# First MLP layer of two chunks with tokens stationary, and a new order of scores and values on TensorE

## The chip, the cores and the metric

The kernel runs on one core of a Trainium2 chip. The metric is the device time of one execution in microseconds; the median over the runs is compared. Inside a core, TensorE (PE for matmuls, PEld for its weight loads), VectorE (DVE), ScalarE (ACT) and GpSimd (POOL) each work through their own instructions in order, and SyncE (SP) issues the DMAs in order. An instruction waits on semaphores for its inputs and for its output buffer.

## The reference, cut to what matters

```python
# q, k, v: (8, 8, 576, 64) float32; w_in: (512, 2048); w_out: (2048, 512)
scores = scale * np.matmul(q, k.transpose(0, 1, 3, 2))          # scale = 1/8
kth = np.partition(scores, -32, axis=-1)[..., -32:-31]
scores = np.where(scores >= kth, scores, -1e9)
scores = scores - np.max(scores, axis=-1, keepdims=True)
attn = np.exp(scores)
attn = attn / (np.sum(attn, axis=-1, keepdims=True) + 1e-09)
x = np.matmul(attn, v)                 # then (batch, seq, heads * 64) = (4608, 512)
h = x @ w_in
out = np.maximum(0.01 * h, h) @ w_out  # (4608, 512)
```

Attention keeps, in each row of 576 scores, the 32 largest; its output goes through a two-layer MLP with a leaky ReLU. The MLP's weights arrive as 64-bit words and are rounded to fp32 on the chip.

## The kernel before

**Units and steps.** Attention is cut into 144 units. A unit is 128 rows of queries of one pair of heads, or the last 64 rows of two pairs. The loop of L416 makes one step per unit, and each step works on several units at different stages: the top-k of unit s on DVE (`top_k`, L209), the mask of unit s-1 on POOL and its exponential on ACT, the normalization of unit s-2 on ACT and its transposition (`transpose`, L252: two copies that split the 16-bit halves, a DMA to DRAM and a transposing DMA back into `wT`). In even steps the scores of units s+2 and s+3 are computed (`scores`, L191) and the values of units s-4 and s-3 (`weigh_values`, L276), which `keep_values` (L290) copies into `x`. DVE's `reciprocals` of a step need the row sums `ze` that ACT makes at the end of the step before.

**MLP.** Tokens are cut into chunks, two of 128 and 17 of 256 (`CHUNKS`, L51). A chunk becomes ready when the values of all its units are there: chunk 0 in step 6, chunk 1 in step 10, chunk 2 in step 18, and then one every 8 steps (`ready_at`). The generator `mlp` (L299) emits a chunk's work in small pieces: for each of 16 groups of 128 hidden features four matmuls with the weights stationary and the tokens moving (`ph`), and a leaky ReLU by ACT into `gT[f]`; then for each 128 tokens 16 matmuls with `gT[f]` stationary (`pz`), a copy and a store. `mlp_steps` is called seven times in each step and takes pieces up to a budget. `slot_budget` (L379) divides the outstanding work, in the costs of `mlp_cost`, by the slots left until the next chunk is ready. So the order on each engine is written out by hand; nothing is reordered later (`tc.manual_schedule`). What ACT has to do for the MLP stands in ACT's queue between the parts of attention.

**Order in an even step on TensorE.** Five slots of MLP, the scores of the first new unit, the values of two units, the scores of the second new unit, two slots of MLP.

**PSUM.** There are 8 banks. Scores have two tiles `psc0` and `psc1` of two banks, one for each of the unit's heads, and both units of an even step use the same two. Values have one bank (`po`), the MLP three in turn (`ph`, `pz`). An fp32 matmul appears in the profile as two records.

**Tile shapes.** MLP matmuls use all 128 rows and 128 columns of the array, scores 64 rows (the head's dimension) and 128 columns, two heads in different rows, and values 128 rows and 64 columns, two heads in different columns.

**Rounding.** Before the loop, 16 pieces of weights are rounded, in three overlapped stages (`round_weights`, L103): ACT copies the parts out of the words, DVE makes scale and mantissa and TensorE sums the parts in PSUM, DVE multiplies. For odd pieces ACT makes `scale` (L127), for even ones DVE (L131). The loop of L400 also emits the loads of q and k, and at `n == NPIECE - 2` the scores of units 0 and 1.

Of the kernel before, what the change touches and what calls it, by code (L numbers as in the profile page):

```python
# [8 lines left out]
F32 = mybir.dt.float32  # L9
U32 = mybir.dt.uint32  # L10
U16 = mybir.dt.uint16
# [8 lines left out]
def kernel(  # L20
# [24 lines left out]
    B = NPAIR // HP  # L45
    HS = S // 2
    NFC = DFF // P
    WCH = 1024
# [14 lines left out]
    ps_sc = ctx.enter_context(tc.tile_pool(name="ps_sc", bufs=1, space=bass.MemoryType.PSUM))  # L63
    ps_po = ctx.enter_context(tc.tile_pool(name="ps_po", bufs=1, space=bass.MemoryType.PSUM))
    ps_ml = ctx.enter_context(tc.tile_pool(name="ps_ml", bufs=3, space=bass.MemoryType.PSUM))

# [8 lines left out]
    w_out = [const.tile([P, 4, DMODEL], F32, name=f"w_out{c}") for c in range(NFC // 4)]  # L75
    gT = [const.tile([P, CHMAX], F32, name=f"gT{f}") for f in range(NFC)]

# [25 lines left out]
    def round_weights(n):  # L103
# [21 lines left out]
        nc.vector.tensor_scalar(scale, scale, 1151.0, 896.0, ALU.min, ALU.max)  # L125
        if n % 2:
            nc.scalar.activation(scale, scale, AF.Copy, bias=-896.0 * 128, scale=128.0)  # L127
        nc.vector.tensor_scalar(m_top, top, 0xF, 0x3F80, ALU.bitwise_and, ALU.bitwise_or)
        nc.vector.tensor_scalar(top, top, 0x8000, None, ALU.bitwise_and)
        if n % 2 == 0:  # L130
            nc.vector.tensor_scalar(scale, scale, 896.0, 128.0, ALU.subtract, ALU.mult)  # L131
        if n < NPIECE - 3:
            pw = ps_sc.tile([P, 2, 512], F32, name=f"psc{n % 2}")
            sums = [(pw[:, h, :], h * 512) for h in range(2)]
            ends = [(pw.rearrange("p h n -> p (h n)"), 0)]
        else:
            ends = sums = [(ps_ml.tile([P, 512], F32, name="pw", tag="ml"), h * 512) for h in range(2)]
# [52 lines left out]

    def scores(u):  # L191
        ps = [ps_sc.tile([P, 2, 512], F32, name=f"psc{i}") for i in range(2)]
        for n in range(0, len(u.parts), 2):
            for half in range(2):
                for i, pi, side, r0 in u.parts[n:n + 2]:
                    qt, kt = qk_of[pi]
                    d = slice(side * D, (side + 1) * D)
                    nc.tensor.matmul(  # L198
                        ps[i][r0:r0 + u.rows, half, 0:HS],
                        qt[d, u.q0:u.q0 + u.rows],  # L200
                        kt[d, half * HS:(half + 1) * HS],
                        start=True, stop=True,
                    )
        u.both = work.tile([P, 2, S], F32, name="s_sb", bufs=5)
        u.s = [u.both[:, i, :] for i in range(2)]
        for i in range(2):
            nc.scalar.copy(u.s[i].rearrange("p (h n) -> p h n", h=2), ps[i][:, :, 0:HS])  # L207

# [81 lines left out]
    def keep_values(u, po):  # L290
# [5 lines left out]
        for o, (pi, _, _) in enumerate(u.outs):  # L296
            nc.scalar.copy(x_of[ch][pi % HP][:, col:col + n], po[:, o, :])  # L297

    def mlp(ch):  # L299

        n = CHUNKS[ch]
        t0 = sum(CHUNKS[:ch])
        x = x_of[ch]
        for f in range(NFC):
            ph = ps_ml.tile([P, 512], F32, name="ph", tag="ml")
            for c in range(HP):
                nc.tensor.matmul(  # L307
                    ph[:, 0:n], w_in[c][:, f * P:(f + 1) * P], x[c][:, 0:n],
                    start=(c == 0), stop=(c == HP - 1),
                )  # L310
                if c == 1:
                    yield 2 * max(n, 225)
            nc.scalar.activation(gT[f][:, 0:n], ph[:, 0:n], AF.Prelu, alpha=SLOPE)  # L313
            yield 2 * max(n, 225)
        for r0 in range(0, n, P):
            m = min(P, n - r0)
            pz = ps_ml.tile([P, 512], F32, name="pz", tag="ml")
            for f in range(NFC):
                nc.tensor.matmul(  # L319
                    pz[0:m, 0:DMODEL], gT[f][:, r0:r0 + m], w_out[f // 4][:, f % 4, :],  # L320
                    start=(f == 0), stop=(f == NFC - 1),
                )
                if f % 2 and f + 1 < NFC:
                    yield 2 * DMODEL
# [5 lines left out]
    def mlp_cost(ch):  # L330
        n = CHUNKS[ch]
        return NFC * HP * max(n, 225) + -(-n // P) * NFC * DMODEL

# [45 lines left out]
    def slot_budget(s):  # L379

        after = [at for at, _ in ready_at if at >= s]
        until = after[0] if after else s
        return backlog[0] / ((until + 1 - s) * SLOTS)

    SLOTS = 7

    with tc.manual_schedule():
# [12 lines left out]
        for n in range(NPIECE + 2):  # L400
# [6 lines left out]
            if 6 <= n < 6 + HP:  # L407
                load_qk(n - 6)
            elif n == NPIECE - 2:
                for u in steps[0:2]:  # L410
                    scores(u)
            elif n == NPIECE - 1:
                load_v(0)
                load_v(1)

        for s in range(len(steps) + LAG + 1):  # L416
# [29 lines left out]
            if old:  # L446
                exponents(old, 1)
                sums(old)
            for u in new[:1]:
                scores(u)  # L450
            if s % 2 == 0:
                po = ps_po.tile([P, 2, P], F32, name="po")
                for values in (weigh_values, keep_values):
# [3 lines left out]
                attended(s)  # L457
            for u in new[1:]:
                scores(u)
            budget = slot_budget(s + 1)  # L460
# [62 lines left out]
```

## Time and profile before

| What | Value |
|---|---|
| Median of 9 runs | 1516.41 us (1515.33 to 1518.45) |
| Profiled execution: time / span | 1518.21 us / 1516.4 us |
| Busy PE, DVE, ACT, POOL | 1430.6, 1330.6, 1117.7, 1078.1 us |
| PE L307 (first layer), L319 (second layer) | 519.7, 506.7 us |
| PE L198 (scores), L283 (values) | 198.2, 180.3 us |
| ACT L313 (leaky ReLU), L207 (copies of scores), L259 (splits) | 107.1, 169.3, 315.7 us |
| Idle of PE before L198, waiting for L207 | 29.8 us, the longest 23.4 |
| Idle of DVE, waiting for `ze` | 75.2 us in 48 places |
| Mean granted TensorE clock | 0.973 |

The span goes from the first to the last instruction. A matmul's recorded time contains its passage through the array, so records overlap: the distance between starts tells what one costs. A group is named by line, engine, operation and output<-inputs; a wait is put down to what ended it.

### The profile page before, as it was taken

The page shows a single profiled execution, that of the slowest core. Times are in us where ns is not written, and L with a number is a line of the kernel's source. Part 1 is how long each engine was busy: PE and PEld are TensorE (multiplying, and loading weights), DVE is VectorE, ACT ScalarE, POOL GpSimd, SP SyncE. Part 2 cuts the span into 40 slices and gives each one's busy share as a digit, 9 for nine tenths or more (in the row PEclk, how much of TensorE's full clock was granted, in tenths as well). Part 3 has the DMA queues.
Part 4 walks back from the last instruction along what each step waited for, and adds up shares of the span by engine and source line. Part 5 has one row for each costly group of instructions (what it writes and reads, how often), then busy time and mean ns, then how long its engine had stood idle before and what let it go on. Part 6 is the DMA issues. An engine that isn't in the chain of part 4 may idle for free.

```text
span 1516.4 us, 24441 instructions
## 1 busy us (share of the span) xinstructions
PE 1430.6 (94%) x8192; PEld 952.4 (63%) x8192; DVE 1330.6 (88%) x3421; ACT 1117.7 (74%) x2141; POOL 1078.1 (71%) x726
## 2 busy tenths in 40 slices
PE   6736978999999999999999999999999999999998
PEld 2324665757575767575757676767676666666774
DVE  6799999999999999999999998999999989999600
ACT  7846786878787877687878787878787878787720
POOL 0068778787878777878787877777787878788700
PEclk9966999999999999999999999999999999999999
DMA  7714456555665455545754456555665455544510
GB/s 287 277 31 125 126 162 165 166 141 148 179 159 148 126 170 158 160 137 148 182 165 134 139 158 170 164 136 147 190 158 147 135 158 155 156 130 142 141 53 14
DMA packets 399294, 227.05 MB, mean 150 GB/s; under 512 B 343360, under 2 KB 343360, under 8 KB 397120
## 3 DMA queue, kind: packets, MB, share of 16 engines
q1 hardware_dynamic: 399168, 225.49, 53.5%
q8 instruction: 64, 1.05, 0.3%
q14 instruction: 62, 0.51, 0.1%
HBM read 46.14 MB, written 94.37 MB: 93 GB/s over the span
## 4 chain that ended last, share of the span: by engine, by line
PE 83%; DVE 11%; ACT 3%; DMA 1%; issue 1%; SPq 0%; POOL 0%; DVEq 0%; ACTq 0%; POOLq 0%
PE ph L307 32%; PE pz L319 30%; PE psc L198 10%; PE po L283 10%; DVE tops L221 4%; DVE pairs L224 3%; DVE pairs L216 1%; ACT split L259 1%; DVE scale L144 1%; DVE w_in L147 0%; ACT s_sb L238 0%; ACT s_sb L250 0%; DVE w_out L147 0%; DMA raw<-in_weights_dram 0%; ACT scale L127 0%
## 5 line engine op out<-in xcount | busy, mean ns | idle before, releaser
L234 POOL TENSOR_SCALAR pen<-s_sb,tops 128x576 f32<-128x576 f32 x288 | 637.5, 2214 | 240.2 <-DVE tops L221 204.2
L221 DVE MAX8 tops<-pairs 128x8 f32<-128x288 f32 (+1 forms) x1152 | 635.8, 591 | 0.0
L307 PE MATMUL ph<-x,w_in 128*128 128x256 f32 (+1 forms) x2432 | 519.7, 374 | 6.4 <-ACT gT L313 6.4
L319 PE MATMUL pz<-w_out,gT 128*128 128x512 f32 x1152 | 506.7, 595 | 1.3 <-ACT gT L313 1.3
L307 PEld LDWEIGHTS ph<-x,w_in 128*128 128x128 f32 x2432 | 444.4, 193 | 87.4 <-issue 21.9
L224 DVE MATCH_REPLACE8 pairs<-tops,pairs 128x288 f32<-128x288 f32 (+1 forms) x864 | 460.0, 537 | 0.0
L235 POOL TENSOR_TENSOR s_sb<-s_sb,pen 128x576 f32<-128x576 f32 x288 | 406.4, 1411 | 24.1
L319 PEld LDWEIGHTS pz<-w_out,gT 128*128 128x128 f32 x1152 | 215.9, 190 | 265.5 <-issue 263.0
L259 ACT COPY split<-s_sb 128x1152 uint16<-128x1152 uint16 x288 | 315.7, 1145 | 0.0
L207 ACT COPY s_sb<-psc 128x576 f32<-128x576 f32 x288 | 169.3, 639 | 114.3 <-PE psc L198 114.3
L250 ACT ACTIVATE s_sb<-s_sb,rz 128x576 f32<-128x576 f32 x288 | 206.7, 767 | 35.4 <-DVE rz L247 35.4
L238 ACT ACTIVATE s_sb<-s_sb,nbias 128x576 f32<-128x576 f32 x288 | 221.2, 768 | 11.4 <-POOL s_sb L235 11.4
L198 PE MATMUL psc<-kt,qt 64*128 64x288 f32 (+1 forms) x1280 | 198.2, 438 | 29.8 <-ACT s_sb L207 29.8
L216 DVE TENSOR_TENSOR pairs<-s_sb 128x576 f32<-128x576 f32 x288 | 213.5, 780 | 10.2 <-ACT split L259 0.5
L283 PE MATMUL po<-wT,vt 128*64 128x128 f32 (+1 forms) x3200 | 180.3, 269 | 21.4 <-DMA wT<-apart 20.6
L283 PEld LDWEIGHTS po<-wT,vt 128*64 128x64 f32 x3200 | 161.4, 139 | 53.0 <-issue 27.2
L313 ACT ACTIVATE gT<-ph 128x256 f32<-128x256 f32 (+1 forms) x304 | 107.1, 368 | 102.0 <-PE ph L307 101.6
L198 PEld LDWEIGHTS psc<-kt,qt 64*128 64x128 f32 (+1 forms) x1280 | 111.0, 181 | 101.1 <-ACT s_sb L207 39.0
L232 POOL TENSOR_SCALAR nbias<-tops 128x2 f32<-128x2 f32 x144 | 33.4, 232 | 92.1 <-DVE tops L221 79.3
L247 DVE RECIPROCAL rz<-ze 128x2 f32<-128x2 f32 x144 | 22.4, 156 | 75.7 <-ACT ze L243 75.2
L297 ACT COPY x<-po 128x128 f32<-128x128 f32 (+1 forms) x160 | 32.4, 264 | 63.2 <-PE po L283 63.0
L224 DVE MATCH_VALUE_LOAD pairs<-tops,pairs 128x8 f32 x864 | 62.2, 72 | 0.0
(38 smaller groups left out, 317.8 us busy)
## 6 DMA issues: line engine op xcount, KB each, us to landing
apart<-split SPq DMA_DIRECT2D x288, 288.0 KB, 2.1
raw<-in_weights_dram SPq DMA_DIRECT2D x16, 1024.0 KB, 5.1
vt<-in_vk_dram SPq DMA_DIRECT2D x32, 320.0 KB, 3.7
qt<-in_qT_dram SPq DMA_DIRECT2D x32, 288.0 KB, 3.8
kt<-in_kT_dram SPq DMA_DIRECT2D x32, 288.0 KB, 4.0
out_dram<-o_sb SPq DMA_DIRECT2D x36, 256.0 KB, 2.0
wT<-apart SPq DMA_TRANSPOSE x144, 4.6
```

What stands on the lines that cost most here:

```text
L198: nc.tensor.matmul(ps[i][r0:r0 + u.rows, half, 0:HS], qt[d, u.q0:u.q0 + u.rows], kt[d, half * HS:(half + 1) * HS], start=True, stop=True,)
L216: nc.vector.tensor_tensor(pairs[:, :, n, :], u.both[:, :, 0:HS], u.both[:, :, HS:S], op)
L221: nc.vector.max(out=u.tops[:, i, r, :], in_=rest[i])
L224: nc.vector.match_replace(out=rest[i], in_to_replace=u.tops[:, i, r, :], in_values=rest[i], imm_value=LOWEST)
L234: nc.gpsimd.tensor_scalar(pen, u.s[i], u.tops[:, i, ROUNDS - 1, 7:8], MASKED, ALU.is_lt, ALU.mult)
L235: nc.gpsimd.tensor_tensor(u.s[i], u.s[i], pen, ALU.add)
L238: nc.scalar.activation(u.s[i], u.s[i], AF.Exp, bias=u.nbias[:, i:i + 1], scale=SCALE, accum_out=u.z[:, i:i + 1])
L250: nc.scalar.activation(u.s[i], u.s[i], AF.Copy, bias=0.0, scale=u.rz[:, i:i + 1])
L259: nc.scalar.copy(split, pairs[:, :, h])
L283: nc.tensor.matmul(po[side * D:(side + 1) * D, o, :], vt[:, c, side, :], u.wT[:, c + side * NKC if c + 1 < NKC else c, r:r + n], start=(c ...
L307: nc.tensor.matmul(ph[:, 0:n], w_in[c][:, f * P:(f + 1) * P], x[c][:, 0:n], start=(c == 0), stop=(c == HP - 1),)
L319: nc.tensor.matmul(pz[0:m, 0:DMODEL], gT[f][:, r0:r0 + m], w_out[f // 4][:, f % 4, :], start=(f == 0), stop=(f == NFC - 1),)
```

## The change

Three things are done, and some that they need.

- In `scores`, both units of an even step are computed together. A row's 576 scores are split into 352 (`wide`) and 224 (`narrow`) columns. A unit has a `wide` tile of two banks; both share the two banks of `narrow`. The order on PE is first unit wide, first narrow, second narrow, second wide, and ACT copies in that order. The values' `po` has no bank of its own: it takes a buffer of `wide`, of which there are two. In the even step, values and their copies now come first, then all scores.
- The first layer of chunks 0 and 1 (`hidden_of_few`) has the 128 tokens stationary and 512 weights moving. Its output has tokens in partitions, so after the leaky ReLU TensorE transposes it in blocks of 128x128, and ACT copies four of them at a time into `gT`. `mlp_cost` gives these chunks another cost, and `slot_budget` spreads their work over one step less.
- The scores of units 0 and 1 are emitted one piece later in the rounding loop, behind the copies of the last piece. That piece's `scale` is made by DVE, and where DVE makes it, it now precedes the mantissa.
- The MLP has two PSUM buffers in place of three. For the other chunks one buffer holds two groups of 256 columns and one ReLU evicts both. `gT` is one tile.

```diff
--- before.py
+++ after.py
@@ -44,6 +44,8 @@
     HP = DMODEL // P
     B = NPAIR // HP
     HS = S // 2
+    NARROW = 224
+    WIDE = S - NARROW
     NFC = DFF // P
     WCH = 1024
     LEFT = S % P
@@ -61,8 +63,7 @@
     small = ctx.enter_context(tc.tile_pool(name="small", bufs=5))
     halves = ctx.enter_context(tc.tile_pool(name="halves", bufs=3, space=bass.MemoryType.DRAM))
     ps_sc = ctx.enter_context(tc.tile_pool(name="ps_sc", bufs=1, space=bass.MemoryType.PSUM))
-    ps_po = ctx.enter_context(tc.tile_pool(name="ps_po", bufs=1, space=bass.MemoryType.PSUM))
-    ps_ml = ctx.enter_context(tc.tile_pool(name="ps_ml", bufs=3, space=bass.MemoryType.PSUM))
+    ps_ml = ctx.enter_context(tc.tile_pool(name="ps_ml", bufs=2, space=bass.MemoryType.PSUM))
 
     ident = const.tile([P, P], F32, name="ident")
     make_identity(nc, ident)
@@ -73,7 +74,7 @@
 
     w_in = [const.tile([P, DFF], F32, name=f"w_in{c}") for c in range(HP)]
     w_out = [const.tile([P, 4, DMODEL], F32, name=f"w_out{c}") for c in range(NFC // 4)]
-    gT = [const.tile([P, CHMAX], F32, name=f"gT{f}") for f in range(NFC)]
+    gT = const.tile([P, NFC, CHMAX], F32, name="gT")
 
 
 
@@ -123,14 +124,14 @@
         nc.vector.tensor_scalar(scale, top, 4, 0x7FF, ALU.logical_shift_right, ALU.bitwise_and)
 
         nc.vector.tensor_scalar(scale, scale, 1151.0, 896.0, ALU.min, ALU.max)
-        if n % 2:
+        if n % 2 and n + 1 < NPIECE:
             nc.scalar.activation(scale, scale, AF.Copy, bias=-896.0 * 128, scale=128.0)
+        else:
+            nc.vector.tensor_scalar(scale, scale, 896.0, 128.0, ALU.subtract, ALU.mult)
         nc.vector.tensor_scalar(m_top, top, 0xF, 0x3F80, ALU.bitwise_and, ALU.bitwise_or)
         nc.vector.tensor_scalar(top, top, 0x8000, None, ALU.bitwise_and)
-        if n % 2 == 0:
-            nc.vector.tensor_scalar(scale, scale, 896.0, 128.0, ALU.subtract, ALU.mult)
         if n < NPIECE - 3:
-            pw = ps_sc.tile([P, 2, 512], F32, name=f"psc{n % 2}")
+            pw = ps_sc.tile([P, 2, 512], F32, name="wide", bufs=2)
             sums = [(pw[:, h, :], h * 512) for h in range(2)]
             ends = [(pw.rearrange("p h n -> p (h n)"), 0)]
         else:
@@ -188,23 +189,31 @@
                 for hp in range(0, HP, 2)]
         units += left + whole if first else whole + left
 
-    def scores(u):
-        ps = [ps_sc.tile([P, 2, 512], F32, name=f"psc{i}") for i in range(2)]
-        for n in range(0, len(u.parts), 2):
-            for half in range(2):
+    def scores(us):
+
+
+        narrow = ps_sc.tile([P, 2, 512], F32, name="narrow")
+        ps = {}
+        for k, u in enumerate(us):
+            wide = ps_sc.tile([P, 2, 512], F32, name="wide", bufs=2)
+            ps[u] = ((wide[:, :, 0:WIDE], 0, WIDE),
+                     (narrow[:, :, k * NARROW:(k + 1) * NARROW], WIDE, S))
+
+        order = ((us[0], 0), (us[0], 1), (us[1], 1), (us[1], 0))
+        for u, part in order:
+            to, k0, k1 = ps[u][part]
+            for n in range(0, len(u.parts), 2):
                 for i, pi, side, r0 in u.parts[n:n + 2]:
                     qt, kt = qk_of[pi]
                     d = slice(side * D, (side + 1) * D)
-                    nc.tensor.matmul(
-                        ps[i][r0:r0 + u.rows, half, 0:HS],
-                        qt[d, u.q0:u.q0 + u.rows],
-                        kt[d, half * HS:(half + 1) * HS],
-                        start=True, stop=True,
-                    )
-        u.both = work.tile([P, 2, S], F32, name="s_sb", bufs=5)
-        u.s = [u.both[:, i, :] for i in range(2)]
-        for i in range(2):
-            nc.scalar.copy(u.s[i].rearrange("p (h n) -> p h n", h=2), ps[i][:, :, 0:HS])
+                    nc.tensor.matmul(to[r0:r0 + u.rows, i, :], qt[d, u.q0:u.q0 + u.rows],
+                                     kt[d, k0:k1], start=True, stop=True)
+        for u in us:
+            u.both = work.tile([P, 2, S], F32, name="s_sb", bufs=5)
+            u.s = [u.both[:, i, :] for i in range(2)]
+        for u, part in order:
+            to, k0, k1 = ps[u][part]
+            nc.scalar.copy(u.both[:, :, k0:k1], to)
 
     def top_k(u):
 
@@ -296,28 +305,55 @@
         for o, (pi, _, _) in enumerate(u.outs):
             nc.scalar.copy(x_of[ch][pi % HP][:, col:col + n], po[:, o, :])
 
+    EARLY = 2
+
+    def hidden_of_few(x):
+
+        g_of = {}
+        for j in range(NFC // 4 + 1):
+            if j < NFC // 4:
+                ph = ps_ml.tile([P, 512], F32, name="ph", tag="ml")
+                for c in range(HP):
+                    nc.tensor.matmul(ph, x[c][:, 0:P], w_in[c][:, j * 512:(j + 1) * 512],
+                                     start=(c == 0), stop=(c == HP - 1))
+                    if c == 1:
+                        yield 2 * 512
+                g_of[j] = raws.tile([P, 2 * DMODEL], U16, name="scale", bufs=2).bitcast(F32)
+                nc.scalar.activation(g_of[j], ph, AF.Prelu, alpha=SLOPE)
+                yield 2 * 512
+            if j:
+                pt = ps_ml.tile([P, 4, P], F32, name="pt", tag="ml")
+                for i in range(4):
+                    nc.tensor.transpose(pt[:, i, :], g_of[j - 1][:, i * P:(i + 1) * P], ident)
+                nc.scalar.copy(gT[:, 4 * (j - 1):4 * j, 0:P], pt)
+                yield 2 * P
+
     def mlp(ch):
 
         n = CHUNKS[ch]
         t0 = sum(CHUNKS[:ch])
         x = x_of[ch]
-        for f in range(NFC):
-            ph = ps_ml.tile([P, 512], F32, name="ph", tag="ml")
-            for c in range(HP):
-                nc.tensor.matmul(
-                    ph[:, 0:n], w_in[c][:, f * P:(f + 1) * P], x[c][:, 0:n],
-                    start=(c == 0), stop=(c == HP - 1),
-                )
-                if c == 1:
-                    yield 2 * max(n, 225)
-            nc.scalar.activation(gT[f][:, 0:n], ph[:, 0:n], AF.Prelu, alpha=SLOPE)
+        if ch < EARLY:
+            yield from hidden_of_few(x)
+        for f0 in range(0, NFC if ch >= EARLY else 0, 2):
+            ph = ps_ml.tile([P, 2, CHMAX], F32, name="ph", tag="ml")
+            for i in range(2):
+                f = f0 + i
+                for c in range(HP):
+                    nc.tensor.matmul(
+                        ph[:, i, 0:n], w_in[c][:, f * P:(f + 1) * P], x[c][:, 0:n],
+                        start=(c == 0), stop=(c == HP - 1),
+                    )
+                    if c == 1 or i == 0 and c == HP - 1:
+                        yield 2 * max(n, 225)
+            nc.scalar.activation(gT[:, f0:f0 + 2, 0:n], ph[:, :, 0:n], AF.Prelu, alpha=SLOPE)
             yield 2 * max(n, 225)
         for r0 in range(0, n, P):
             m = min(P, n - r0)
             pz = ps_ml.tile([P, 512], F32, name="pz", tag="ml")
             for f in range(NFC):
                 nc.tensor.matmul(
-                    pz[0:m, 0:DMODEL], gT[f][:, r0:r0 + m], w_out[f // 4][:, f % 4, :],
+                    pz[0:m, 0:DMODEL], gT[:, f, r0:r0 + m], w_out[f // 4][:, f % 4, :],
                     start=(f == 0), stop=(f == NFC - 1),
                 )
                 if f % 2 and f + 1 < NFC:
@@ -329,6 +365,8 @@
 
     def mlp_cost(ch):
         n = CHUNKS[ch]
+        if ch < EARLY:
+            return NFC * DMODEL + NFC // 4 * (HP * 512 + 2 * P)
         return NFC * HP * max(n, 225) + -(-n // P) * NFC * DMODEL
 
     ready, running = [], [None]
@@ -380,7 +418,8 @@
 
         after = [at for at, _ in ready_at if at >= s]
         until = after[0] if after else s
-        return backlog[0] / ((until + 1 - s) * SLOTS)
+        few = len(after) >= len(CHUNKS) - EARLY
+        return backlog[0] / (max(until + 1 - few - s, 1) * SLOTS)
 
     SLOTS = 7
 
@@ -406,10 +445,9 @@
             load_weights(n + 3)
             if 6 <= n < 6 + HP:
                 load_qk(n - 6)
-            elif n == NPIECE - 2:
-                for u in steps[0:2]:
-                    scores(u)
             elif n == NPIECE - 1:
+                scores(steps[0:2])
+            if n == NPIECE - 1:
                 load_v(0)
                 load_v(1)
 
@@ -446,17 +484,15 @@
             if old:
                 exponents(old, 1)
                 sums(old)
-            for u in new[:1]:
-                scores(u)
             if s % 2 == 0:
-                po = ps_po.tile([P, 2, P], F32, name="po")
+                po = ps_sc.tile([P, 2, 512], F32, name="wide", bufs=2)[:, 0, 0:2 * P].rearrange("p (u n) -> p u n", u=2)
                 for values in (weigh_values, keep_values):
                     for n, u in enumerate((unit(s - LAG - 1), unit(s - LAG))):
                         if u:
                             values(u, po[:, n, :])
                 attended(s)
-            for u in new[1:]:
-                scores(u)
+            if new:
+                scores(new)
             budget = slot_budget(s + 1)
             mlp_steps(budget)
             mlp_steps(budget)
```

## Prediction

> **What bounds the kernel now.** I read the page first: the busy times and the 40 slices.
>
> ```profile
> span 1516.4 us, 24441 instructions
> PE 1430.6 (94%) x8192; PEld 952.4 (63%) x8192; DVE 1330.6 (88%) x3421; ACT 1117.7 (74%) x2141; POOL 1078.1 (71%) x726
> ...
> PE   6736978999999999999999999999999999999998
> ...
> DVE  6799999999999999999999998999999989999600
> ...
> PE 83%; DVE 11%; ACT 3%; DMA 1%; issue 1%; SPq 0%; POOL 0%; DVEq 0%; ACTq 0%; POOLq 0%
> ```
>
> There are two regimes. In slices 2 to 5 PE has holes and DVE is full; later PE is full. The busy times by stretch put the border at 256 us:
>
> ```profile
> 78.00:256.00 178.00, 121.22 (x824) 86.04 (x821) 170.43 (x444) 121.95 (x246) 138.06 (x93) 0.81 0.44 125
> 256.00:1500.00 1244.00, 1242.47 (x7196) 838.99 (x7195) 1102.02 (x2870) 932.99 (x1835) 939.36 (x628) 1.00 0.55 147
> ```
>
> The columns are length, then busy PE, PEld, DVE, ACT, POOL, clock, DMA share, GB/s. From 256 us PE idles 1.5 us in 1244: what is cut there counts in full. Before that, top-k on DVE sets the pace. A step (one unit) is 8.86 us of DVE when it isn't held up (starts of steps 0 to 7 in the trace: 78.4, 87.1, 95.9, ... 140.2). Chunk 2's MLP, ready at step 18, begins at 258.2 us, and from there the end is that start plus PE's work. So the sum has two terms: how late step 18 comes, and what PE does afterwards.
>
> **The steady part: fewer turns of the array.** The timeline of PE, around an even step:
>
> ```profile
> 1006.09 1.02 PE L319 MATMUL pz<-w_out,gT 128*128 128x512 f32 x2
> 1007.04 1.24 PE L198 MATMUL psc<-kt,qt 64*128 64x288 f32 x8
> 1008.22 2.40 PE L283 MATMUL po<-wT,vt 128*64 128x128 f32 x40
> 1010.55 1.24 PE L198 MATMUL psc<-kt,qt 64*128 64x288 f32 x8
> 1011.72 0.70 PE L319 MATMUL pz<-w_out,gT 128*128 128x512 f32 x1
> ```
>
> Each tile shape (128\*128, 64\*128, 128\*64) follows another. An fp32 product is two records. By single starts, pz records come every 429 ns, ph 216, a pair of score records 242, a pair of value records 109. At each turn the next start is 90 to 99 ns late and the first record of the new shape lasts 105 ns longer (52 for values). MLP to scores costs 94+105, scores to values 90+52, values to scores 99+105, scores to MLP 96+105: 746 ns per even step. In the new order (MLP, values, both units' scores, MLP) one turn goes: 93+52, 99+105, 96+105 = 550 ns. That is 196 ns x 61 even steps after 256 us = **12.0 us less**. The Trainium skill, "TensorEngine Tiling (Array Packing)", Key Properties, says that a change of tiling mode drains TensorE but that a change of tile doesn't. It is why I charge nothing between the two units' scores; the row gives the price.
>
> The widths 352 and 224 in place of 288 and 288 leave the columns equal: (293+187) x 2 against 240 x 4 ns. A narrow pair (187 ns) still hides a weight load (108 ns between two loads of one side). ACT copies as many elements in as many instructions.
>
> **The second layer's and first layer's PSUM.** Three banks with one 256-column group become two with two groups. A group is 8 x 216 = 1.73 us, so ACT has two groups' time (3.46 us) before PE needs a bank again, before and after. The eviction grows from 380 to about 585 ns (the 128x512 copy of L326), but half of them go: 16 x 380 = 6.1 becomes 8 x 585 = 4.7 us per chunk on ACT. In 16 places a bank came free just in time (140 ns before the matmul), always for an odd-numbered group, where the pair's eviction now stands. Its extra 0.2 us would cost 3 us; but the eviction of the even group before it goes, which held ACT (at 1015.47 the normalization waited 1.43 us behind it). I take 0. The bound is 0 to +3. That gT is now one tile costs nothing if dependencies go by region, as they do for s_sb: at 90.28 us the exponential of its first half starts 40 ns after the add on that half, and 2.4 us before the add on the other.
>
> **What the new order waits for.** Values now stand 1.17 us earlier, ahead of the first unit's scores. Behind a waiting value matmul are all scores and MLP, and no other work of PE can pass it. From each transposing DMA's landing to the first value matmul that needs it I get 0.04 to 3.0 us over 65 units; nine have under 1.17, and their shortfalls sum to 4.3 us. V is late once already:
>
> ```profile
> 634.27 0.80 PE L283 MATMUL po<-wT,vt 128*64 128x64 f32 x20 [0.70 <-DMA vt<-in_vk_dram]
> ```
>
> This stall grows by 1.2 us, and three like places (about 294, 972 and 1310 us, where V lands within 0.7 us of use) might add 0.5 each. ACT reaches its splits earlier where an even group's eviction is gone. Between 0 and +8 I take **+3.5**. In return the second unit's scores no longer wait for the first's copies, but only their wide part for two copies of values (0.44 us), with two narrow parts (0.75 us) and a wide one between. I see at most 0.5 us to gain there after 256 us.
>
> **The startup.** The waits of DVE between 76 and 270 us, then the chain of work from 149 us:
>
> ```profile
> DVE rz L247 <- ACT ze L243: 7.3, 4, 2.7
> ```
> ```profile
> 149.89 1.43 ACT s_sb L250 x2
> 151.31 0.76 ACT s_sb L238 x2
> 152.07 2.10 ACT split L259 x2
> 154.16 0.18 ACT gT L313
> ...
> 154.39 7.25 PE ph L307 x48
> ```
>
> DVE lost 2.0, 1.2 and 2.7 us in steps 8, 10 and 12 and 0.4 in 17: the MLP of the first two chunks comes late on PE, ACT waits for it in order, and the row sums (ze) that DVE's reciprocal needs stand behind it on ACT. The new form hardly saves PE time: before, 128 records at 112 ns = 14.3 us per chunk; after, 32 at 429 = 13.7, plus 16 transposes. I take these at 0.11 us each (a weight load's spacing), so 15.5. The skill's "TensorE: Matmul & The Clock Gate", Part 4, gives about 275 ns in a kernel, and says that transposes don't raise the clock: 18.1 us. ACT goes from 16 x 272 = 4.4 to 8 x 585 = 4.7 us. And the budget crowds chunk 0: from four steps to three (29 us of PE plus 2.35 per step for scores and values = 12 per step, against DVE's 8.86), with two banks that first-layer groups and transposes take in turn.
>
> Walked by hand with the rows above, at the old times: scores end at 145.4 (both units now precede the MLP), group 0 at 148.9 if the clock is full from 145.6, 150.6 if from 149.0 as in the old run. ACT then evicts, normalizes (1.4), evicts group 1, exponent (0.95), split (2.1), transposes' copy (0.5), exponent, sums: ze at 157.8 to 159.5, where it was 155.65. Step 8 so loses 4.1 to 5.9 us. Group 3 waits for the bank of group 2, ze of step 8 is 2.6 late. The second layer waits for the copies of the transposes behind the next split, with values and scores of step 8 queued behind it: step 10 misses its scores by 2 to 4 us and its ze by 2. That is 11 to 13, and 0 to 1.4 in chunk 1, against 6.3 before: +4.7 to +8. Two gains: scores behind the rounding's copies let ACT begin the last piece at 68.8 in place of 71.6, of which PE's order (both units' scores ahead of the last piece's sums, two banks for three) leaves about 0.7 us; moving scale to DVE in the last piece is in that. And at step 18 PE's scores wait less for ACT and the o_sb copy is out of the way: 1.8 us. The startup is **+3.5** (+2.2 to +5.4 by the walk; -2.5 if the crowding costs nothing).
>
> **Sum.** -12.0 + 3.5 + 3.5 = -5.0. The profiled execution took 1518.2 us for a span of 1516.4; the median of the runs is 1516.4. Taken from the median: **1511.4 us**.
>
> **Rivals.** (1) As summed, 1506 to 1517: 0.47. (2) The startup is no worse and the waits for wT are taken up by ACT's lighter load: -12.0 - 2.5 + 0.5 gives 1502. For it: only 4 waits of DVE, DVE otherwise free to run ahead; 0.18. (3) A wait takes the place of the turn: values wait in 20 steps or more, 8 us with V, startup +3.5: 1516; for it are the margins, against it that ACT's load falls; 0.17. (4) Slower: the clock stays at half through chunk 0. The page's clock was 0.50 to 0.64 from 95 to 152 us. Each of the four groups then takes 6.9 in place of 3.4 us, ACT waits in order for each, and DVE with it: +13.7 on top of the walk's warm case, partly under other waits, so +9: about 1521; beyond +8.5 us of startup the gain is gone. Against it: PE is busy without a hole from 138.8 us. 0.14. (5) gT's reads wait for the whole tile: the last eviction, some 2 us after the last ph, 17 times: 1545; 0.7 us each would decide. 0.04.
>
> **Range and chances.** Cases 2 to 4 span 1502 to 1521 and, with the walk's upper bounds, 1523. The 0.2% that a measurement of this kernel can tell is 3 us. Faster: all of (2) and most of (1), 0.59. Same: the rest of (1) and most of (3), 0.21. Slower: (4), (5) and the rest of (3), 0.20. The likeliest case alone: 1506 to 1517.
>
> **What would show it.** After: three shapes' turns per even step, with po first after MLP, and 16 score records in about 2.2 us; PE's idle after 256 us up from 1.5 to some 5 us, with wT and vt as releasers; DVE's waits for ze early above 7.3 us, with one for scores near step 10; step 18 at 247 to 251 in place of 244.4 us. Wrong would be: step 18 not later (case 2), DVE steps of 12 us before it (4), pz waiting for gT in each chunk (5), or value groups that wait in most steps (3).

## The result, and the profile after

The changed kernel takes 1507.34 us (median of 9 runs, 1506.01 to 1510.27). The kernel before, with the runs that were timed beside it, takes 1515.82 us (29 runs, 1513.01 to 1518.45). The ratio is 0.9944, with a 95% interval of 0.9936 to 0.9952: 8.5 us faster, where 5.0 were forecast. The profiled execution took 1508.37 us, 9.9 less than that of before. The sum of the prediction is therefore held against these 9.9 us, since all the lines come from these two executions.

The page after, first the span and the busy times, then PE's 40 slices, then the shares of the chain that ended last:

```profile
span 1506.5 us, 24058 instructions
PE 1401.3 (93%) x8032; PEld 929.7 (62%) x8032; DVE 1334.0 (89%) x3422; ACT 1111.0 (74%) x1988; POOL 1078.3 (72%) x726
...
PE   5624887999999999999999999999999999999998
...
PE 81%; DVE 7%; DMA 5%; ACT 5%; issue 1%; SPq 0%; DVEq 0%; ACTq 0%
```

The picture is the same as before: PE is full from slice 8 on. PE has 160 records less, and 29.3 us less of busy time. But busy time alone doesn't say where the 9.9 us are. The busy times by stretch (columns as in the prediction):

```profile
78.00:256.00 178.00, 114.32 (x626) 63.33 (x624) 163.77 (x423) 119.26 (x220) 130.85 (x88) 0.81 0.41 115
256.00:1490.00 1234.00, 1225.89 (x7243) 841.60 (x7244) 1111.63 (x2893) 931.16 (x1711) 946.74 (x633) 1.00 0.55 150
```

In the first stretch DVE did 163.8 us of work, 6.7 less than before: attention got less far in the same time. In the second, PE idles 8.1 us where it idled 1.5; 5.4 of these lie ahead of chunk 2's MLP.

**Two terms.** The prediction cut the time at the first matmul of chunk 2's MLP. In the traces this is at 258.2 us before and at 268.2 us after, so the start-up became **10.0 us longer**. From there to the last matmul there are 1253.8 us before (258.2 to 1512.0) and 1234.0 us after (268.2 to 1502.1), so the steady part became **19.8 us shorter**. (The second number is the firmer one. In six of the seven runs with the changed kernel's steady part, its length lies between 1232.7 and 1234.2 us; in the seventh it is 1237.2. The start-up of a single trace is less sure: one run below, whose code is the kernel before's up to step 20, reaches chunk 2's MLP at 254.4 us and not at 258.2.) Both terms had the sign that was forecast, and both are larger: +3.5 was forecast for the first (with the values' waits apart), -12.0 + 3.5 for the second.

**Inside the steady part** I took the starts of PE's records. The MLP at the spacings of the prediction (216 ns for `ph`, 429 for `pz`) makes 936.3 us in both kernels. The rest are 64 blocks of scores and values, each with its turns of the array (what the matmuls around it lose by the turn included): 314.6 us before, 297.7 after. What is left over is 2.9 and -0.1 us. So the blocks gave 16.9 us and the MLP 3.0. Of the MLP's 3.0 about 1.7 are its first records before, which ran at half clock (0.50 up to 261.6 us). Another 0.9 are four places before where a first-layer group waited for its bank, behind a split on ACT (490.2, 793.7, 1093.9 and 1394.5 us, 0.23 us each); after, no such place is left.

This is a block after, in the timeline of PE (start, length, engine, line, what it makes, count of records):

```profile
1000.40 2.31 PE L355 MATMUL pz<-w_out,gT 128*128 128x512 f32 x5
1002.64 2.40 PE L292 MATMUL wide<-wT,vt 128*64 128x128 f32 x40
1004.98 0.86 PE L209 MATMUL wide<-kt,qt 64*128 64x352 f32 x4
1005.67 0.92 PE L209 MATMUL narrow<-kt,qt 64*128 64x224 f32 x8
1006.43 0.76 PE L209 MATMUL wide<-kt,qt 64*128 64x352 f32 x4
1007.12 0.70 PE L355 MATMUL pz<-w_out,gT 128*128 128x512 f32 x1
```

There are three turns, as the change says, and the 16 score records take 1007.12 - 1004.98 = 2.14 us. Such a block is 4.67 us; the commonest one before was 4.87. That is 0.20 us less, the predicted price of a turn (196 ns), and over 61 blocks 12.2 us.

**The larger find is in the blocks that were not common.** Before, 15 of the blocks took 5.24 us. In 11 of them the second unit's scores took 1.60 us in place of 1.24, 0.37 us more for the block. In four, where the values are 80 records and a block is otherwise 5.02 us, they cost 0.22. One more block (1250.5 us) lost 0.70. Together this is 4.0 + 0.9 + 0.7 = 5.6 us, and after it is gone. One of the 11 before, in PE's timeline and then in ACT's:

```profile
1029.24 1.60 PE L198 MATMUL psc<-kt,qt 64*128 64x288 f32 x8
1030.78 0.48 PE L307 MATMUL ph<-x,w_in 128*128 128x256 f32 x1
```
```profile
1028.29 0.20 ACT L243 ACTIVATE ze<-z 128x2 f32<-128x2 f32 x1
1028.40 1.16 ACT L207 COPY s_sb<-psc 128x576 f32<-128x576 f32 x2
```

The 8 records take 1.60 us here and 1.24 in the prediction's timeline. Scores of the two heads use different rows of the array and run side by side. Here the second unit's first head starts at 1029.24, but its second head only at 1029.6: its bank (`psc1`) was free only when ACT's second copy ended at 1029.56. From then on the two heads ran displaced, and their ends too. This wait doesn't show as idle time of PE, because the other head was running. In the list of waits before it stands only as the weight loads' (PEld), with 2.3 us in 13 places of at most 0.2 us.

**Inside the start-up.** The waits of DVE between 76 and 270 us after (what waited and its line, what ended the wait, then sum, count and longest in us):

```profile
DVE rz L256 <- ACT ze L252: 5.6, 3, 3.1
DVE pairs L225 <- ACT s_sb L216: 5.1, 1, 5.1
```

These are 10.7 us against 6.3 in the same steps before: 3.1, 2.1 and 0.5 us for `ze` in steps 8, 9 and 10, and 5.1 for the scores in step 10. The walk had said steps 8 to 10, scores and `ze`, 11 to 13 us. One cost in the 5.1 it had not named. The second layer of chunk 0 stands ahead of step 8's values and scores on PE, and its first 8 records ran at half clock, after the wait for `gT` (granted clock 0.50 from 168.1 to 174.9 us):

```profile
169.51 6.37 PE L355 MATMUL pz<-w_out,gT 128*128 128x512 f32 x8 [4.00 <-ACT gT L328]
```

At 429 ns a record they would take 3.4 us and not 6.3. So by estimate some 2.8 us of the 5.1 are the clock.

Top-k begins at 81.5 us (before: 78.4) and step 18 at 253.0 (244.4), so that the first 18 steps take 171.5 in place of 166.0 us, **+5.5**, and the rounding ahead of them **+3.1**. (Another run of the same rounding code can end it earlier: top-k begins at 79.8 to 80.3 us in three of the runs below, so the +3.1 is the upper end of 1.4 to 3.1.) From step 18 to chunk 2's MLP it is 15.2 us (13.8), **+1.4**. The chain of work there, from the view of what ended last:

```profile
245.47 6.56 DMA apart<-split
252.09 4.67 DMA wT<-apart
256.90 1.33 PE wide L292 x20
258.24 4.42 DMA wT<-apart
262.70 2.39 PE wide L292 x19
```

The write of `apart` took 6.6 us from issue to landing, against a median of 2.1; four loads of q and k were issued just ahead of it (243.0 to 244.5 us), and whether they made it late isn't tested. The transposition behind it came late, its values waited 1.9 us, the next transposition began when these values had ended, and the values that complete chunk 2's tokens waited another 4.5 us. PE's list of waits after 256 us has these two and those of the steady part in one line:

```profile
PE wide L292 <- DMA wT<-apart: 8.0, 6, 4.5
```

So four places with 1.7 us are left for the steady part, and one for `vt` (1.1 us): 2.8 us, against 1.5 before. With what follows a wait in its block, values lose 3.9 us there after and 2.0 before, **+2**. Late loads of q and k cost scores 1.3 us before (1.2 of it at 577.0 us) and 0.3 after. With 12.1 us for the turns, these sum to about the 16.9: 12.1 + 5.6 - 1.9 + 1.0.

### The profile page after: what moved, and what is told of

Its sections match the earlier page's. It is cut to its first block, busy times and chain, and to the rows that moved or that the text cites. A ratio compares the mean times of both kernels' runs of the same rounds, so it can differ in the third digit from the quotient of the medians.

```text
span 1506.5 us, 24058 instructions
## 1 busy us (share of the span) xinstructions
PE 1401.3 (93%) x8032; PEld 929.7 (62%) x8032; DVE 1334.0 (89%) x3422; ACT 1111.0 (74%) x1988; POOL 1078.3 (72%) x726
## 4 chain that ended last, share of the span: by engine, by line
PE 81%; DVE 7%; DMA 5%; ACT 5%; issue 1%; SPq 0%; DVEq 0%; ACTq 0%
PE ph L343 30%; PE pz L355 29%; PE wide L292 10%; PE wide L209 6%; PE narrow L209 3%; DMA wT<-apart 2%; DVE tops L230 2%; DVE pairs L233 2%; DMA apart<-split 2%; ACT split L268 2%; ACT s_sb L259 1%; DVE pairs L225 1%; ACT s_sb L247 1%; DMA raw<-in_weights_dram 1%; PE ph L317 1%
## 5 line engine op out<-in xcount | busy, mean ns | idle before, releaser
L343 PE MATMUL ph<-x,w_in 128*128 128x256 f32 x2176 | 481.1, 381 | 0.0
L343 PEld LDWEIGHTS ph<-x,w_in 128*128 128x128 f32 x2176 | 410.7, 190 | 77.4 <-issue 23.7
L292 PE MATMUL wide<-wT,vt 128*64 128x128 f32 (+1 forms) x3200 | 183.2, 271 | 61.0 <-DMA wT<-apart 60.0
L292 PEld LDWEIGHTS wide<-wT,vt 128*64 128x64 f32 x3200 | 163.0, 140 | 104.1 <-ACT s_sb L247 35.4
L306 ACT COPY x<-wide 128x128 f32<-128x128 f32 (+1 forms) x160 | 32.2, 260 | 152.5 <-PE wide L292 152.4
L349 ACT ACTIVATE gT<-ph 128x512 f32<-128x512 f32 x136 | 80.7, 593 | 80.9 <-PE ph L343 80.9
L216 ACT COPY s_sb<-wide 128x704 f32<-128x704 f32 x144 | 108.7, 755 | 31.2 <-PE wide L209 31.1
L209 PE MATMUL wide<-kt,qt 64*128 64x352 f32 (+1 forms) x640 | 120.4, 496 | 0.3 <-ACT x L306 0.3
L216 ACT COPY s_sb<-narrow 128x448 f32<-128x448 f32 x144 | 69.6, 536 | 4.1 <-PE narrow L209 3.4
L209 PE MATMUL narrow<-kt,qt 64*128 64x224 f32 (+1 forms) x640 | 69.4, 359 | 0.8 <-DMA kt<-in_kT_dram 0.8
```

The costliest lines, as they stand in the source:

```text
L209: nc.tensor.matmul(to[r0:r0 + u.rows, i, :], qt[d, u.q0:u.q0 + u.rows], kt[d, k0:k1], start=True, stop=True)
L292: nc.tensor.matmul(po[side * D:(side + 1) * D, o, :], vt[:, c, side, :], u.wT[:, c + side * NKC if c + 1 < NKC else c, r:r + n], start=(c ...
L343: nc.tensor.matmul(ph[:, i, 0:n], w_in[c][:, f * P:(f + 1) * P], x[c][:, 0:n], start=(c == 0), stop=(c == HP - 1),)
```

## Experiments

Theory A, the prediction's: a turn costs 0.2 us and gives the steady gain, and the crowding of chunk 0 costs the start-up. Theory B: the gain comes from something else in the order of scores. Theory C: the new form or the rounding makes the start-up late. All ratios are to the kernel before, on the same chip; the changed kernel's is 0.9944. Not all runs were on one chip, so they are compared by these ratios. "Steady part" and "block" are measured as above.

### The form of the first layer: weights stationary again

```diff
-    EARLY = 2
+    EARLY = 0
```

This takes the new form away from chunks 0 and 1, and with it their new cost and the step that `slot_budget` took from them. All else of the change stays.

> The changed kernel, with the first layer of chunks 0 and 1 as in the kernel before (weights stationary, old cost, four steps of budget). If the new form of that layer is what held DVE back in steps 8 to 10 (10.7 us of waits, against 6.3 before), these waits return to about 6 us, step 18 comes some 4 to 5 us earlier than 253.0 us, and the time is about 1503 us. If the form pays for itself on TensorE and the late start has another cause, the time stays at 1507 us or rises.

Measured: 1499.56 us, ratio 0.9898 (0.9884 to 0.9911). Step 18 is at 243.1 us, the chunk 2 MLP at 257.2, and the steady part is the changed kernel's, 1234.2. DVE's wait for `ze` in the start-up:

```profile
DVE rz L256 <- ACT ze L252: 3.1, 2, 1.8
```

Of 10.7 us of waits 3.1 are left, and the wait for scores is gone. This is more than the expectation took back (1503 us). So this part of the change, form and budget together, costs 0.9944 - 0.9898 = 0.0046 of the time, 7 us. The next run tells which of the two.

### The new form with the old spread

```diff
-        few = len(after) >= len(CHUNKS) - EARLY
+        few = 0
```

> The changed kernel, but chunks 0 and 1 spread over as many steps as before (the budget's one step less is undone). If crowding chunk 0 into three steps is what costs, the waits of DVE in steps 8 to 10 fall from 10.7 us to 6 to 8 and the time to 1503 to 1505 us. If it is the form (transposes and first-layer groups that take turns in two banks), the waits stay within 2 us and the time at 1506 to 1508 us.

Measured: 1499.95 us, ratio 0.9903 (0.9890 to 0.9917). Step 18 at 246.2, chunk 2's MLP at 260.9, steady part 1233.4.

```profile
DVE rz L256 <- ACT ze L252: 4.8, 5, 1.7
```

With the form kept, the same time comes back as without it, and again more than was expected. The one step less that the budget gives to chunk 0 and 1 is what makes the first 18 steps late. Between these two runs the form makes no difference (0.9898 and 0.9903). In both, the wait of values ahead of chunk 2's MLP is also shorter, 2.0 and 2.2 us at most in place of 4.5.

### The rounding: piece 13 in the scores' banks

The rounding ended 3.1 us later, against a forecast of 0.7 us earlier. PE's timeline after, at its end (a bracket gives the idle time before and what ended it):

```profile
70.80 0.59 PE L141 MATMUL pw<-wT,ident_top 128*128 128x512 bf16 x1 [4.02 <-DVE w_out L148]
71.18 1.91 PE L142 MATMUL pw<-w_out,ident 128*128 128x512 f32 x2
...
76.00 0.86 PE L209 MATMUL wide<-kt,qt 64*128 64x352 f32 x4
78.14 0.39 PE L141 MATMUL pw<-wT,ident_top 128*128 128x512 bf16 x1
```

The last three pieces are summed in the MLP's buffers. A piece takes two, and there are now two in place of three. So piece 14 waits 4.0 us until DVE has multiplied piece 13. From 69.1 us, in this hole, to 75.9 us the granted clock is at half, and the two records at 71.18 take 1.91 us. The scores at 76.0 and then the sums of the last piece at 78.14 stand behind all of this. The edit lets piece 13 use a `wide` buffer:

```diff
-        if n < NPIECE - 3:
+        if n < NPIECE - 2:
```

> The changed kernel, with the sums of piece 13 of the rounding in a wide buffer in place of the MLP's two banks, so that piece 14's sums needn't wait for piece 13's products. If that wait (4.0 us of TensorE at 70.8 us, after which the clock was at half) makes the rounding end late, top-k starts at 78 to 79 us in place of 81.5 and the time falls by about 3 us, to 1504. If the order of scores ahead of the last piece's sums is the cause, top-k starts within 0.7 us of 81.5 us and the time stays.

Measured: 1503.93 us, ratio 0.9927 (0.9915 to 0.9939). Top-k begins at 78.0 us. The same place in PE's timeline:

```profile
67.86 0.38 PE L141 MATMUL pw<-wT,ident_top 128*128 128x512 bf16 x1 [1.43 <-DVE wT L131]
68.08 1.02 PE L142 MATMUL pw<-w_out,ident 128*128 128x512 f32 x2
70.53 0.86 PE L209 MATMUL wide<-kt,qt 64*128 64x352 f32 x4
```

The wait for a buffer is gone, the two records take 1.02 us, and the scores run 5.5 us earlier. The start of top-k is back where it was before the change. In the time it is about 2.6 us; the two intervals just touch, so that the gain rests on the trace more than on the time.

### The first scores one piece earlier again

```diff
-        if n % 2 and n + 1 < NPIECE:
+        if n % 2:
...
-            elif n == NPIECE - 1:
+            elif n == NPIECE - 2:
                 scores(steps[0:2])
-            if n == NPIECE - 1:
+            elif n == NPIECE - 1:
```

> The changed kernel, with the first scores back at their old place in the rounding (one piece earlier) and the last piece's scale back on ACT. If the move behind the rounding's copies is a gain, ACT starts the last piece some 2.5 us later than at 70.0 us again, and top-k starts at 82 to 84 us: 1508 to 1510 us in all. If the move is itself what put top-k at 81.5 us in place of 78.4, top-k starts at 78 to 79.5 us and the time is 1504 to 1505 us.

Measured: 1505.25 us, ratio 0.9940 (0.9927 to 0.9954). Top-k begins at 78.1 us, as early as with piece 13 elsewhere. In the total it is not told apart from the changed kernel. Here the scores run at 65.8 us, in the time in which PE would stand still; piece 14's wait is 1.9 us, and the clock stays full up to 84.1 us. So neither the lack of a buffer nor the move of the scores makes the rounding late alone: undoing either one is enough. Together they put top-k at 79.8 to 81.5 us in the five traces that have both, since the scores then stand between piece 14's sums, which come late, and piece 15's. (The run also puts the last piece's `scale` back on ACT; the two were not taken apart.) The prediction had booked the move as a gain of 0.7 us.

### The kernel before, with the copies out of the way

This is theory B alone. The kernel before keeps its four turns, banks and form. In the even steps that had the long blocks (the third and fourth even step of every eight) the first unit's scores, and with them their copies on ACT, are emitted ahead of the exponential and the sums, and no longer behind them:

```diff
+            early = s % 8 in (4, 6) and s > 18
+            if early:
+                for u in new[:1]:
+                    scores(u)
             if old:
                 exponents(old, 1)
                 sums(old)
-            for u in new[:1]:
+            for u in new[:1] if not early else ():
                 scores(u)
```

> The kernel before, where only ACT's order is changed, and only in the even steps whose MLP work is first-layer groups: the copies of the first unit's scores stand ahead of the second half's exponential and the row sums. If in these steps the second unit's scores waited for the first unit's copies, their block on TensorE (turns included) falls from 5.24 us to about 4.87 and the time by up to 0.36 x 31 = 11 us, to 1505; it is less where the later row sums hold DVE. If the gain of the change in the steady part is turns of the array alone, the block and the time stay (1513 to 1518 us).

Measured: 1507.18 us, ratio 0.9948 (0.9933 to 0.9962). PE's timeline at one of these steps:

```profile
1015.59 1.24 PE L198 MATMUL psc<-kt,qt 64*128 64x288 f32 x8
...
1019.10 1.24 PE L198 MATMUL psc<-kt,qt 64*128 64x288 f32 x8
1020.27 3.94 PE L307 MATMUL ph<-x,w_in 128*128 128x256 f32 x17
```

The second unit's 8 records (at 1019.10) take 1.24 us and not 1.60. No block of 5.24 us is left, and the sum of the blocks falls from 314.6 to 308.2 us, by 6.4. Of these, 4.9 are second scores that no longer wait for the copies; the other 1.5 are blocks where V, or q and k, came sooner here, which is not known to be the edit's doing. So the copies that came late on ACT had cost about 5 us in these steps, and moving one call in the kernel before takes 7.5 us off the time, nearly the whole change's 8.5. (The steady part falls by 8.1. The 1.7 beside the blocks are a stretch of half clock, 254.8 to 261.6 us, that in the trace of before reaches 3.4 us into it; in this run the last such stretch, 234.5 to 237.9 us, ends ahead of it.) The expectation allowed for all 31 steps in question; 15 had been long.

### The new order alone, on the old banks

In the kernel before, values come first and then both units' scores, still on the shared `psc0` and `psc1`:

```diff
-            for u in new[:1]:
-                scores(u)
             if s % 2 == 0:
                 po = ps_po.tile([P, 2, P], F32, name="po")
...
-            for u in new[1:]:
+            for u in new:
                 scores(u)
```

> The kernel before with values ahead of both units' scores and nothing else: one turn fewer, but the second unit's scores need the very banks that the first's copies must clear. If the banks matter, the second unit waits some 1.3 us in every even step, the block of values and scores grows from 4.87 to about 5.9 us and the time to 1570 to 1590 us. If the order alone carries the gain, the block is 4.67 us and the time about 1503 us.

Measured: 1606.46 us, ratio 1.0601 (1.0574 to 1.0627), above the expected range. PE's timeline:

```profile
1006.06 1.24 PE L198 MATMUL psc<-kt,qt 64*128 64x288 f32 x8
1008.02 1.77 PE L198 MATMUL psc<-kt,qt 64*128 64x288 f32 x8 [0.72 <-ACT s_sb L207]
1009.73 0.48 PE L307 MATMUL ph<-x,w_in 128*128 128x256 f32 x1
```

Without the values between them, the second unit's scores wait 0.72 us for the first's copies and then run displaced (1.77 us); a block takes 6.2 us. The expectation had this mechanism, with 5.9. One turn fewer on the old banks thus costs far more than it saves. The new split into `wide` and `narrow` is what makes the order possible.

### A turn measured by itself

In the changed kernel, one more small matmul in front of the values, in the second bank of the buffer that `po` takes. In one kernel it has the scores' tile shape (64 rows, 128 columns), which adds a turn, in the other the values' shape, which adds none. Its result isn't used.

```diff
-                po = ps_sc.tile([P, 2, 512], F32, name="wide", bufs=2)[:, 0, 0:2 * P].rearrange("p (u n) -> p u n", u=2)
+                both = ps_sc.tile([P, 2, 512], F32, name="wide", bufs=2)
+                po = both[:, 0, 0:2 * P].rearrange("p (u n) -> p u n", u=2)
+                if unit(s - LAG - 1):
+                    nc.tensor.matmul(both[:, 1, 0:D], ident[0:D, :], ident[0:D, 0:D], start=True, stop=True)    # one more turn
+                    nc.tensor.matmul(both[0:D, 1, 0:D], ident[:, 0:D], ident[:, 0:D], start=True, stop=True)    # same shape
```

(Each kernel has one of the two last lines.)

> The changed kernel with one small matmul more ahead of the values of each even step, 64 rows by 128 columns with 64 moving columns: it puts one more turn between MLP and values. Its own two records are about 0.11 us. If a turn costs 0.2 us, the block grows by 0.3 us and the time by 70 x 0.3 = 21 us, to about 1528 us. If turns are free, by 8 us, to 1515. To be read beside the run with a same-shaped matmul.

> The same with the small matmul in the shape of the values (128 rows by 64 columns, 64 moving columns), so that no turn is added: the block grows by its own 0.11 us, the time by about 8 us, to 1515. The difference to the run with one more turn is the turn's price: 14 us if it is 0.2 us, nothing if turns are free.

Measured: 1527.85 us with the turn, ratio 1.0082 (1.0065 to 1.0099), and 1513.40 us without, ratio 0.9995 (0.9986 to 1.0005). PE's timeline with the turn:

```profile
1013.15 1.02 PE L355 MATMUL pz<-w_out,gT 128*128 128x512 f32 x2
1014.11 0.43 PE L491 MATMUL wide<-ident 64*128 64x64 f32 x2
1014.47 2.40 PE L292 MATMUL wide<-wT,vt 128*64 128x128 f32 x40
```

The difference is 14.45 us, 0.24 us for each of 61 blocks; blocks take 5.03 and 4.78 us. The small matmul in the values' shape costs 0.11 us (4.78 - 4.67), as expected. So a turn costs 0.24 to 0.25 us here, somewhat more than the 0.20 of the change and the 196 ns of the prediction's rows.

### Two parts of the start-up undone together

```diff
-        if n < NPIECE - 3:
+        if n < NPIECE - 2:
...
-    EARLY = 2
+    EARLY = 0
```

> The changed kernel with both startup losses undone: weights stationary for chunks 0 and 1 (with the old budget), and piece 13 of the rounding in a wide buffer. Alone they gave about 6.7 and 2.4 us less than the changed kernel (by the ratios to the kernel before). If the two add, the ratio is 0.9898 - 0.0016 = 0.988 and the time 1497 us, with top-k starting at 78 us and chunk 2's MLP at about 254 us. If TensorE's clock or another wait takes one of them back, it stays at 0.990.

Measured: 1495.03 us, ratio 0.9876 (0.9857 to 0.9894). Top-k begins at 77.5 us, step 18 at 239.4, chunk 2's MLP at 252.3.

```profile
252.00:1480.00 1228.00, 1223.56 (x7197) 837.86 (x7194) 1101.71 (x2868) 924.18 (x1698) 938.48 (x627) 1.00 0.55 149
```

PE idles 4.4 us in this stretch. This is the best version: 1.2% faster than the kernel before and 0.7% faster than the changed one.

The companion keeps the form and takes piece 13 elsewhere and the old spread:

```diff
-        if n < NPIECE - 3:
+        if n < NPIECE - 2:
...
-        few = len(after) >= len(CHUNKS) - EARLY
+        few = 0
```

> The same, but with the tokens stationary for chunks 0 and 1 and only the budget as before. If the crowding and not the form of that layer cost the time, this is within 1 us of the other run of this call, about 1497 us; if the transposes cost on TensorE or ACT once the rest is out of the way, it is 2 to 4 us slower.

Measured: 1499.14 us, ratio 0.9893 (0.9879 to 0.9908), step 18 at 244.6, chunk 2's MLP at 259.5. This is 4.1 us above the run before, and not within 1 us of it: it is the expectation's other branch, by which the form costs something. In its trace DVE waits 6.7 us for `ze` in the start-up, where the run before has 2.3. But the two intervals overlap a little, and the first two runs of this section were 0.4 us apart. Whether the form costs a few us in the start-up, or nothing, stays open.

## Why the prediction was right, and where its sizes were off

The forecast was faster by 5.0 us, and it became faster by 8.5. Held against the profiled executions (9.9 us), the sum hides two misses of opposite sign. The main mechanism, the turns, is shown. That the total came within 3.5 us is in part luck, since a gain that wasn't booked (11.3 us) and a loss that wasn't booked (6.5) cancel in part.

- **Turns, -12.0: right.** The commonest block is 0.20 us shorter, and the measurement of a turn by itself gives 0.24.
- **"At most 0.5 us to gain" from the second unit's scores: the step that failed most.** It was 5.6 us, and moving the copies in the kernel before showed 4.9 of it alone. I had taken the waits that the list shows as what the copies cost. But a late bank for one head costs the overlap of both heads, 1.60 in place of 1.24 us, and PE stays busy all along.
- **Values' waits, +3.5: too high.** It is about +2. The long waits are there in the steady part (`wT` in 4 places, V in one), but few, and the stall for V grew by 0.36 us (0.70 to 1.06) and not by 1.2.
- **First and second layer's PSUM in the steady part, 0: right for what it speaks of.** No `pz` waits for `gT` after the first chunks, and the MLP doesn't run slower. It runs 3.0 us faster: 1.7 by the place of the half clock, and 0.9 because beside the places where a bank came just in time there were four before where it came late, and after there is none. (The pairs' eviction and the single `gT` tile were not tested alone.)
- **The crowding of chunk 0, +4.7 to +8: right, with one cost not seen.** It is +5.5, in the steps and at the waits that were walked, and the old spread gives it back (6 us less in all). The bound from rows held because each wait was followed to the engine that comes late next. But the walk had step 10's scores late by 2 to 4 us, and they were late by 5.1, of which the half clock in the second layer makes some 2.8 by estimate.
- **The rounding's end, -0.7: wrong, +3.1.** The walk saw that ACT would start its last piece earlier (it does, 70.0 in place of 71.6 us), and priced "two banks for three" at less than that gain. It didn't follow what a piece with two buffers does to the next one: a wait of 4.0 us, then a half clock, with the scores in front of the last sums. Up to 1.7 us of it differs from run to run with the same code.
- **Step 18, -1.8: wrong, +1.4.** The scores did stop waiting (2.3 us before), but the values then waited 1.9 and 4.5 us for `wT`, behind a write of `apart` that landed late. Step 18 itself came at 253.0 us, past the 247 to 251 that were forecast.

In sum: the steady part was forecast at -8.5 and is -19.8; the start-up was forecast at +3.5 and is +10.0. Of the 11.3 us of difference in the steady part the copies make 5.6, the values 1.6, the late q and k 1.0 and the MLP 3.0. Of the 6.5 in the start-up the rounding makes 3.8 and step 18 another 3.2; the walk's own part is 0.5 below what was taken for it (5.5 against 6.0).

**The rivals.** Values that wait in place of the turn (1516 us): not so, they wait in 5 places and not in 20. The clock at half through chunk 0 (1521 us): it was full from 147.6 to 168.1 us, so that chunk 0's first-layer groups ran at the full rate; it came true only for the start of the second layer. (The argument against it, that PE is busy without a hole from 138.8 us, overlooked a wait of 0.8 us that ended at 141.9 us before.) Reads of `gT` that wait for the whole tile (1545 us): PE waits 4.0 us for it in the whole run, all in the first chunks. A start-up that is no worse (1502 us): it is 10 us worse, and only the larger steady gain brings the time near. The time lies between the likeliest case and this one for a reason that neither had.

## What to carry to other kernels

Where TensorE is full, count the changes of tile shape in the loop: one cost 0.20 to 0.25 us here, measured in two ways. Where two matmuls share the array side by side, look at the starts of both before you trust the list of waits: a late bank for one of them cost 0.36 us a time and showed as almost no idle time. And when a PSUM buffer is taken away, walk every phase that uses the pool, the preparation too; here nearly all time lost ahead of the stage that is full was added to the end (its length stayed within 1.5 us in six traces while its start moved by 11, from 257.2 to 268.2 us; in a seventh it was 3 us longer).

## What the runs showed of the hardware that was not expected

- Two heads' scores in different rows of the array, started 0.36 us apart, finish later by about the same amount (1.60 against 1.24 us for 8 records). In these blocks the overlap wasn't made up.
- The transposes of 128x128 fp32 on TensorE start 109 ns apart. This is the 0.11 us that was taken, so that the other estimate in the prediction, 18.1 us for a chunk, was too high. The mean length of one record is 278 ns, with its passage through the array. Each is one record, where a product in fp32 has two:

```profile
L327 PE MATMUL pt<-ident,scale 128*128 128x128 f32 x32 | 5.0, 278 | 2.0 <-ACT scale L322 1.1 <-ACT gT L328 1.0
```
